# Turning q by VectorE in 32x32 blocks, one load per batch, in a linear attention followed by a softplus MLP

## The chip, the cores and the metric

The kernel runs on one core of a Trainium2 chip. The core has five engines with queues of their own: TensorE (PE in the profile, with its weight loads as PEld), VectorE (DVE), ScalarE (ACT), GpSimd (POOL) and SyncE (SP), which here issues nearly all transfers. Sixteen DMA engines move data between the device's memory and the core's memory. The metric is the device time of one execution in microseconds (us), as a median of several runs.

## The reference

```python
# q, k, v: (8, 8, 576, 64) = batch, head, row, column
kv = np.einsum('bhsd,bhse->bhde', k, v)
out = np.einsum('bhsd,bhde->bhse', q, kv)
rms = np.sqrt(np.mean(out * out, axis=-1, keepdims=True) + 1e-06)
out = out / rms * g_norm
x = out.transpose(0, 2, 1, 3).reshape(4608, 512)
h = x @ w_in                                               # (4608, 2048)
g = np.maximum(h, 0.0) + np.log1p(np.exp(-np.abs(h)))      # softplus
return g @ w_out                                           # (4608, 512)
```

The two weights arrive as 64-bit floats; all else is 32-bit. Each batch has 576 rows, that is four and a half tiles of 128 rows.

## The kernel before

**Tiles.** The 4608 rows are 36 tiles of 128. Three tiles make a block of 384 rows, so there are 12 blocks. The 2048 columns of the inner layer are 16 chunks of 128.

**Exactness.** Products of the MLP are made from three rounded factors of each operand, so each logical product is three matmuls. The factors of a weight (`divide`) and of x (`split`) are made by ScalarE and VectorE in turn: a high part, a low part, and a third that is combined from both.

**Attention.** `kv_of(b)` loads k and v of a batch and multiplies them on TensorE (L479), then copies the result block-diagonally into `kv_diag`: one half by ScalarE (L486), the other by VectorE (L487). `rows(t)` treats a tile of 128 rows: q is loaded with one row per partition (L401), turned by TensorE in four 128x128 transposes into the `tp` bank (`turn_q`, L497), copied by ScalarE into `qT` (L522), multiplied by `kv_diag` (`out_rows`, L503), squared by ScalarE (L527), summed by VectorE (L507), epsilon added by VectorE (L508), raised to the power -1/2 on Pool (L511), and multiplied by VectorE (L514). For the first six tiles (`AT_ONCE`) x is then turned by TensorE (`turn_x`, L519) and split at once out of PSUM; ScalarE also copies it (L535) to be stored (L536). For all other tiles VectorE turns x in blocks of 32x32 (L544) and four transfers with runs of 32 floats store it so that it lies fully turned in device memory (L547). Later phases load it again (L556, `x_again`) and split it.

**Steps.** A step is one block with one chunk. `step(s)` makes h by 12 matmuls (`mm1`, L578), softplus on ScalarE (L598), a high part (L600, ScalarE), a low part and a third (L589 and L593, VectorE), and nine matmuls into the three sums of the block (`mm2`, L585). There are 192 steps, in three phases set by `ENDS`: in each phase every block does its share of chunks. Between phases the sums are stored (L629) and added back (L623, L625). `PLACES` = 8 chunks of weights fit at a time; a weight whose place comes free too late is converted early and spilled to device memory (`w_spill`, L330).

**Order.** Nothing is scheduled by hand. Every piece of work is a `Task` with an engine, an estimated time, what it follows, a position, and the slots of rings (buffers) that it takes and gives back. `Plan.order` simulates the engines and picks for each the task with the smallest position among those that could start soon; the programs of all engines are written out in that order. Positions come from the step number and from the 40 numbers of `P0` (when weights are fetched and converted, how far ahead x, k, v and q are worked on). The rings say how many buffers there are: two for q, three for gv, two for sq. Each engine runs its list strictly in order, and so does SP with its transfers, each of which waits on SP until its buffer is free. While the first step is not reached, the plan fills idle time of TensorE with matmuls of no use (`warm`, L683).

## Time and profile before

| | |
|---|---|
| median of 5 runs | 926.32 us (926.02 to 927.71) |
| the profiled execution | 926.02 us, its span 924.2 us |
| granted TensorE clock | 1.00 |
| TensorE busy | 911.6 us of the span |
| VectorE busy | 624.9 us |
| ScalarE busy | 441.9 us |
| Pool busy | 64.0 us |
| transfers by SP's queue | 132.68 MB, 51.4% of the 16 engines' span |

A line of a group names the line of the program, the engine, the operation, what is written and read, the shape and the count; then busy time, mean duration in ns, the idle time of the engine just ahead of it and who ended that. A line of a timeline gives the start in us from the start of the span, the duration, and the same names; `x8` are eight like instructions in a row. Matmuls overlap, so what one costs is seen from one start to the next. A transpose of fp32 counts as one matmul, and an ordinary fp32 product as two (160 products with k and v stand as 320).

### The profile page before, as it was taken

The numbers are of one execution on the slowest core, as the hardware profiler recorded it, in microseconds if no ns is written. First come the engines' busy times: TensorE is split into PE (matmuls) and PEld (weight loads), VectorE is DVE, ScalarE is ACT, GpSimd is POOL, SyncE is SP. The second block draws the span as 40 slices with busy tenths as digits, with TensorE's granted clock in tenths as the row PEclk, the third lists the DMA queues.
The fourth block names the chain that finished last, engine by engine and source line by source line (L and its number), as shares of the span: only waits on it lengthen the run. The fifth ranks groups of instructions, "written<-read, shape, count | busy, mean of one in ns | idle before, by whom it ended". The sixth has DMA issues, their size and how long they took to land.

```text
span 924.2 us, 13404 instructions
## 1 busy us (share of the span) xinstructions
PE 911.6 (99%) x4897; PEld 825.0 (89%) x4897; DVE 624.9 (68%) x1075; ACT 441.9 (48%) x843; POOL 64.0 (7%) x42
## 2 busy tenths in 40 slices
PE   7999999999999999999999999999999999999998
PEld 5799899999999999999999989999999999999997
DVE  6988859886567764778688887584455555454553
ACT  5877547665445444655556453353333333333231
POOL 0322311111210220000000000000000000000000
PEclk9999999999999999999999999999999999999999
DMA  9998798676666634333455565522333333332221
GB/s 247 232 253 207 187 228 204 175 175 155 162 162 190 145 87 123 95 111 118 157 171 160 174 203 173 169 98 86 103 103 103 102 103 103 103 103 85 81 76 67
DMA packets 248033, 133.53 MB, mean 144 GB/s; under 512 B 149152, under 2 KB 220832, under 8 KB 247968
## 3 DMA queue, kind: packets, MB, share of 16 engines
q1 hardware_dynamic: 247808, 132.68, 51.4%
q8 instruction: 38, 0.62, 0.3%
q14 instruction: 27, 0.22, 0.1%
q10 hardware_dynamic: 160, 0.00, 0.0%
HBM read 92.80 MB, written 39.85 MB: 144 GB/s over the span
## 4 chain that ended last, share of the span: by engine, by line
PE 97%; DVE 1%; ACT 1%; DMA 0%; issue 0%; ACTq 0%; DVEq 0%
PE h L578 44%; PE s L585 43%; PE o L503 3%; PE o L479 3%; PE tp L497 2%; DMA g_col<-in_g_norm_dram 0%; PE s L503 0%; PE tp L519 0%; PE h L683 0%; DVE t L295 0%; PE h L363 0%; PE h L362 0%; DVE p L308 0%; DVE w L311 0%; ACT L649 0%
## 5 line engine op out<-in xcount | busy, mean ns | idle before, releaser
L578 PE MATMUL h<-xv,w 128*128 128x384 f32 x2304 | 436.1, 338 | 0.0
L585 PE MATMUL s<-w,gv 128*128 128x512 f32 x1728 | 432.9, 394 | 0.0
L578 PEld LDWEIGHTS h<-xv,w 128*128 128x128 f32 x2304 | 405.2, 188 | 14.1 <-issue 0.7
L585 PEld LDWEIGHTS s<-w,gv 128*128 128x128 f32 x1728 | 320.4, 188 | 58.1 <-DVE gv L593 0.2
L598 ACT ACTIVATE g<-h 128x384 f32<-128x384 f32 x192 | 94.3, 491 | 352.1 <-PE h L578 350.1
L589 DVE TENSOR_TENSOR gv<-g,gv 128x384 fp32r<-128x384 f32 x192 | 106.7, 556 | 173.0 <-ACT gv L600 172.4
L593 DVE SCALAR_TENSOR_TENSOR gv<-gv 128x384 fp32r<-128x384 f32 x192 | 106.9, 557 | 5.8
L600 ACT ACTIVATE gv<-g 128x384 fp32r<-128x384 f32 x192 | 100.8, 525 | 7.9 <-PE s L585 2.6
L419 DVE SCALAR_TENSOR_TENSOR xv<-xt,g_col,xv 128x512 fp32r<-128x512 f32 x102 | 76.2, 747 | 19.0 <-ACT xv L416 18.8
L416 ACT ACTIVATE xv<-xt,g_down 128x512 fp32r<-128x512 f32 x102 | 72.4, 713 | 26.8 <-DMA xt<-x 26.6
L511 POOL TENSOR_TENSOR r<-r,half 128x8 f32<-128x8 f32 x36 | 63.3, 1758 | 276.9 <-DVE r L508 276.9
L423 DVE SCALAR_TENSOR_TENSOR xv<-xv 128x512 fp32r<-128x512 f32 x108 | 74.5, 690 | 3.0
L479 PEld LDWEIGHTS o<-kvt,kvt 128*128 128x128 f32 x256 | 33.4, 196 | 4.7 <-issue 3.5
L479 PE MATMUL o<-kvt,kvt 128*128 128x128 f32 x256 | 34.7, 280 | 3.0 <-DMA kvt<-in_v_dram 3.0
L503 PE MATMUL o<-kv_diag,qT 128*128 128x128 f32 (+1 forms) x296 | 36.9, 276 | 0.0
L503 PEld LDWEIGHTS o<-kv_diag,qT 128*128 128x128 f32 (+1 forms) x296 | 34.5, 180 | 1.5 <-issue 0.7
L507 DVE TENSOR_REDUCE r<-x 128x8 f32<-128x512 f32 x36 | 24.4, 678 | 16.1 <-ACT x L527 15.9
L522 ACT COPY qT<-tp 128x512 f32<-128x512 f32 x36 | 21.0, 582 | 27.0 <-PE tp L497 26.9
L625 DVE SCALAR_TENSOR_TENSOR qT<-s,kvt 128x512 f32<-128x512 f32 x36 | 24.6, 687 | 13.7 <-PE s L585 9.8
L625 DVE SCALAR_TENSOR_TENSOR qT<-s,scale,kvt 128x512 f32<-128x512 f32 x12 | 9.0, 752 | 29.5 <-PE s L585 29.5
L527 ACT ACTIVATE x<-o 128x512 f32<-128x512 f32 x33 | 19.7, 596 | 16.3 <-PE o L503 14.4
L295 DVE SCALAR_TENSOR_TENSOR t<-sq,t 128x512 f32<-128x512 bf16 x32 | 22.1, 690 | 5.3 <-ACT sq L279 3.7
(71 smaller groups left out, 482.7 us busy)
## 6 DMA issues: line engine op xcount, KB each, us to landing
xt<-x SPq DMA_DIRECT2D x102, 256.0 KB, 3.3
kvt<-part SPq DMA_DIRECT2D x72, 256.0 KB, 4.3
part<-xg SPq DMA_DIRECT2D x36, 256.0 KB, 2.5
part<-qT SPq DMA_DIRECT2D x36, 256.0 KB, 2.4
raw<-in_moe_w_in_dram SPq DMA_DIRECT2D x16, 512.0 KB, 4.6
kvt<-in_k_dram SPq DMA_DIRECT2D x64, 128.0 KB, 4.3
kvt<-in_v_dram SPq DMA_DIRECT2D x32, 256.0 KB, 4.4
raw<-in_moe_w_out_dram SPq DMA_DIRECT2D x16, 512.0 KB, 4.6
```

Of the source, the lines that this page charges most:

```text
L416: nc.scalar.activation(cols(0, F32R), x.tile, func=AF.Identity, scale=g_down)
L419: nc.vector.scalar_tensor_tensor(out=cols(1, F32R), in0=x.tile, scalar=g_col, in1=cols(0), op0=ALU.mult, op1=ALU.subtract)
L423: nc.vector.scalar_tensor_tensor(out=cols(2, F32R), in0=cols(1), scalar=-RADIX, in1=cols(0), op0=ALU.mult, op1=ALU.add)
L479: nc.tensor.matmul(kv[:, i if tail else p], lhsT=l, rhs=r, start=(p == 0 and i == 0), stop=tail, skip_group_check=True)
L503: nc.tensor.matmul(pairs(y[r0:r0 + n], p), lhsT=qT.tile[:, p, r0:r0 + n], rhs=kv_diag[b % 2][:, p], start=(p == 0), stop=True, skip_group_ ...
L511: nc.gpsimd.tensor_tensor(out=r.tile, in0=r.tile, in1=half, op=ALU.pow)
L578: nc.tensor.matmul(hp, lhsT=w_in.tile[:, i, kd * P:(kd + 1) * P], rhs=xv.tile[:, i, kd], start=(m == 0), stop=(m == 3 * KD - 1))
L585: nc.tensor.matmul(mine[i].tile, lhsT=gv.tile[:, m, i * P:(i + 1) * P], rhs=w_out.tile[:, m], start=(c == cs[0] and m == 0), stop=(c == cs ...
L589: nc.vector.tensor_tensor(out=gv.tile[:, 1], in0=g.tile, in1=gv.tile.bitcast(F32)[:, 0], op=ALU.subtract)
L593: nc.vector.scalar_tensor_tensor(out=gv.tile[:, 2], in0=f32[:, 1], scalar=-RADIX, in1=f32[:, 0], op0=ALU.mult, op1=ALU.add)
L598: a = add("ACT", 490, lambda: nc.scalar.activation(new(g, [P, NT]), h.tile, func=AF.Softplus, scale=1.0 + E), [a], s, [g], [h])
L600: a = add("ACT", 530, lambda: nc.scalar.activation(new(gv, [P, 3, NT], F32R)[:, 0], g.tile, func=AF.Copy, scale=DOWN), [a], s, [gv])
```

## The change

- **q.** For the first two batches q is loaded as before in natural order, but with the heads paired differently (head p with head p + 4), and turned by TensorE. From the third batch on (`b >= 2`) a batch's q is loaded as a whole by four transfers (`load_q`), each into 32 partitions and with runs of 32 floats (128 bytes, where the old runs had 256), so that the 32x32 blocks lie where the turned matrix wants them. VectorE then turns the blocks of a tile in one instruction straight into `qT`. One buffer `qa` holds a batch; the ring of two row tiles is gone. The first two batches' tiles lie in `qa` and in `kvt` slots. A tile across two batches is turned in two parts.
- **Heads.** With the new pairing, k is loaded by halves, and the matmuls of `out_rows` write two strips of 64 columns each.
- **kv_diag.** Both halves are copied by ScalarE.
- **Epsilon** is added on Pool ahead of the power.
- **x.** TensorE turns x of 12 tiles (`BY_PE`) instead of 6. The six new ones are still split after a reload from device memory, but their store has runs of 512 bytes and is one transfer instead of four.
- **Phases.** `ENDS` and the positions in `P0` are new; the bound for spilling is 12 steps instead of 30; gv has two buffers and sq one. Tasks can be made to follow the start of another (`follows`).

```diff
-    ENDS = [[0] * n_blocks, [4] * LATE + [6] * (n_blocks - LATE), [10] * n_blocks, [KF] * n_blocks]
+    ENDS = [[0] * n_blocks, [4]*4+[6]*8, [8]*4+[11]*8, [KF] * n_blocks]
...
-    P0 = [-53.0, -6.2, -18.3, -1.2, -9.1, 4.0, -38.9, 0.2, -43.0, -32.8, -31.7, -14.2, -15.7, -21.2,
-          2.8, -3.7, 1.0, -9.5, 7.0, 7.0, 7.0, 24.5, -0.5, 2.5, 2.0, 16.5, -13.0, 4.5, 16.5, 21.5, 27.0,
-          42.5, 44.0, 66.5, 72, 80, 88, 96.5, 102.0, 3]
+    P0 = [-44.5, 1.3, -27.8, -10.7, -15.1, 4.5, -20.4, -2.8, -54.5, -31.8, -31.7, -9.2, -25.2, -1.2,
+          27.3, -6.2, 3.0, -12.0, 8.5, 9.5, 5.0, 21.5, -1.5, 2.5, 2.5, 27.0, -6.5, 13.0, 9.0, 44.5,
+          49.5, 67.5, 56.5, 71.5, 95.5, 100.5, 115.0, 112.0, 116.5, 9.0]
+    BY_PE = 12
...
-    rings = dict(xv=2, gv=3, g=2, raw=2, lf=1, sq=2, t=1, p=1, w=1,
-                 tail0=1, tail1=1, xt=2, kvt=6, q=2, qT=2, x=2, xg=2, r=2,
+    rings = dict(xv=2, gv=2, g=2, raw=2, lf=1, sq=1, t=1, p=1, w=1,
+                 tail0=1, tail1=1, xt=2, kvt=6, qa=1, qT=2, x=2, xg=2, r=2,
...
-        if c < PLACES or first_step[c] - last_step[c - PLACES] > 30:
+        if c < PLACES or first_step[c] - last_step[c - PLACES] > 12:
...
+    def load_q(b):
+        q_slots[b], q_loads[b] = slot("qa"), []
+        pos = x_pos(first_tile[b] + 1) - EARLY[7]
+        def run(e, c):
+            if not (e or c):
+                new(q_slots[b], [P, NP * S])
+            r0 = BL * (2 * e + c)
+            nc.sync.dma_start(
+                out=q_slots[b].tile[r0:r0 + BL].rearrange("j (i d) -> j i d", d=BL),
+                in_=q[b, e * NP:(e + 1) * NP, :, BL * c:BL * (c + 1)].rearrange("p (i j) d -> j (p i) d", j=BL))
+        for e in range(2):
+            for c in range(2):
+                q_loads[b].append(add("SP", 450, lambda e=e, c=c: run(e, c), (), pos + 0.2 * (2 * e + c),
+                                      [q_slots[b]] if not (e or c) else [], [], 2000, behind=int(pos) - 3,
+                                      follows=q_loads[b][-1] if e or c else None))
...
-            add("DVE", 430, lambda: nc.vector.tensor_copy(kvd[D:, :, D:], bank.tile[D:, :, 1]), [last] + old, pos + 2.5, [], [bank])]
+            add("ACT", 360, lambda: nc.scalar.copy(kvd[D:, :, D:], bank.tile[D:, :, 1]), [last] + old, pos + 2.5, [], [bank])]
...
-                    nc.tensor.matmul(pairs(y[r0:r0 + n], p), lhsT=qT.tile[:, p, r0:r0 + n], rhs=kv_diag[b % 2][:, p],
+                    nc.tensor.matmul(y[r0:r0 + n, p::NP], lhsT=qT.tile[:, p, r0:r0 + n],
+                                     rhs=kv_diag[b % 2][:, p].rearrange("r (h d) -> r h d", d=D),
...
-            nc.vector.tensor_scalar(out=r.tile, in0=r.tile, scalar1=EPS, scalar2=None, op0=ALU.add)
         def root():
+            nc.gpsimd.tensor_scalar(out=r.tile, in0=r.tile, scalar1=EPS, scalar2=None, op0=ALU.add)
             nc.gpsimd.tensor_tensor(out=r.tile, in0=r.tile, in1=half, op=ALU.pow)
...
-        a = add("PE", 440, turn_q, [ld], pos - 1, [tp], [q_s])
-        a = add("ACT", 590, lambda: nc.scalar.copy(new(qT, [P, NP, P]), tp.tile), [a], pos - 1, [qT], [tp])
+        for b, r0, n, s0 in parts(t):
+            if b >= 2:
+                if b not in q_slots:
+                    load_q(b)
+                turned.append(add(
+                    "DVE", 690 if n == P else 420, lambda b=b, r0=r0, n=n, s0=s0: nc.vector.transpose(
+                        out=part_of_qT(n, r0),
+                        in_=q_slots[b].tile.rearrange("k (p s) -> k p s", p=NP)[:, :, s0:s0 + n]),
+                    q_loads[b], pos - 1, [qT] if not r0 else [], [q_slots[b]], follows=turned[-1] if turned else None))
+                continue
...
-        if t < AT_ONCE:
+        if t < BY_PE:
             a = add("PE", 440, turn_x, [a], pos + 0.5, [xp], [x])
-            split(0, t, xp, a, pos + 0.5)
+            if t < AT_ONCE:
+                split(0, t, xp, a, pos + 0.5)
...
-        ot = slot("xg" if ph == 0 else ("qT", "x", "q")[t % TB] if ph == LAST else "qT")
+        ot = slot("xg" if ph == 0 else ("qT", "x", "xg")[t % TB] if ph == LAST else "qT")
```

## Prediction

> **What bounds the kernel now.** I read the page's head first, then the chain, the groups, a table by stage, and the timeline of the start.
>
> ```profile
> span 924.2 us, 13404 instructions
> PE 911.6 (99%) x4897; PEld 825.0 (89%) x4897; DVE 624.9 (68%) x1075; ACT 441.9 (48%) x843; POOL 64.0 (7%) x42
> PE 97%; DVE 1%; ACT 1%; DMA 0%; issue 0%; ACTq 0%; DVEq 0%
> PE h L578 44%; PE s L585 43%; PE o L503 3%; PE o L479 3%; PE tp L497 2%; DMA g_col<-in_g_norm_dram 0%; PE s L503 0%; PE tp L519 0%; PE h L683 0%; DVE t L295 0%; PE h L363 0%; PE h L362 0%; DVE p L308 0%; DVE w L311 0%; ACT L649 0%
> ```
>
> The chain that ends last is TensorE for 97% of the span, so work taken from TensorE is worth its full price and work on other engines costs nothing until TensorE must wait for it. L497, the turning of q, stands on that chain with 2%. The prices, from the groups:
>
> ```profile
> L497 PE MATMUL tp<-ident_r,q 128*128 128x128 f32 x144 | 21.7, 273 | 1.7 <-DVE xv L419 1.0 <-PE h L363 0.4 <-ACT qT L522 0.3
> L522 ACT COPY qT<-tp 128x512 f32<-128x512 f32 x36 | 21.0, 582 | 27.0 <-PE tp L497 26.9
> L544 DVE STREAM_TRANSPOSE xg<-x 128x512 f32<-128x512 f32 x30 | 21.2, 708 | 5.6 <-DMA x<-xg 5.2
> L508 DVE TENSOR_SCALAR r<-r 128x8 f32<-128x8 f32 x36 | 6.2, 172 | 1.2
> L511 POOL TENSOR_TENSOR r<-r,half 128x8 f32<-128x8 f32 x36 | 63.3, 1758 | 276.9 <-DVE r L508 276.9
> masks.py:199 POOL TENSOR_SCALAR_AFFINE_SELECT kv_diag<-kv_diag 128x128 f32<-128x128 f32 x1 | 0.3, 292 | 0.1
> ```
>
> Matmuls overlap, so what a turn costs TensorE is read from starts. In the timeline around 224 us:
>
> ```profile
> 221.79 2.45 PE L585 MATMUL s<-w,gv 128*128 128x512 f32 x10
> 224.08 0.60 PE L497 MATMUL tp<-ident_r,q 128*128 128x128 f32 x4
> 224.51 1.06 PE L479 MATMUL o<-kvt,kvt 128*128 128x128 f32 x8
> ```
>
> The reader should see 224.08 to 224.51: four transposes hold TensorE for 0.43 us, not 4 x 273 ns. The start is another regime:
>
> ```profile
> 0.00:20.00 20.00, 14.17 (x64) 10.33 (x64) 12.60 (x25) 10.95 (x20) 0.70 (x6) 1.00 0.91 240
> 20.00:40.00 20.00, 17.44 (x115) 13.62 (x114) 17.50 (x32) 16.13 (x33) 5.39 (x3) 1.00 1.04 255
> 80.00:100.00 20.00, 20.00 (x117) 17.60 (x116) 18.58 (x35) 12.53 (x25) 5.75 (x4) 1.00 0.67 165
> ```
>
> ```profile
> 41.42 0.71 PE L683 MATMUL h<-ident_r 128*128 128x512 f32 x2
> 42.05 2.32 PE L578 MATMUL h<-xv,w 128*128 128x384 f32 x12
> ...
> 41.74 0.69 DVE L423 SCALAR_TENSOR_TENSOR xv<-xv 128x512 fp32r<-128x512 f32 x1
> ```
>
> The first fence is the table by stage (stretch, length, then busy time of PE, PEld, DVE, ACT, POOL, clock, DMA share, GB/s), the second the timeline of the start. From 20 to 40 us VectorE is busy 17.5 of 20 us, ScalarE 16.1, and the DMA engines are full. The first step (L578) starts at 42.05 us, just as VectorE makes the last factor it needs (L423, from 41.74). Useful TensorE work before that is 16.2 us (the groups at their start-to-start times); the rest is waiting, padded by warming matmuls (L683). After 42 us TensorE never visibly waits, apart from one wait of 0.6 us and some 80 ns at changes of kind.
>
> **The change, part by part, against the profiled execution's 926.02 us** (span 924.2 and 1.8 around it; the median of the five runs, 926.32, is 0.3 higher).
>
> *TensorE work.* Turning q took 36 groups of four; 8 full ones and 2 of half width stay (two batches, with the tile on their border turned in two halves). That is 27 fewer. Six tiles of x more are turned by TensorE: +6. Net 21 x 0.43 = 9.0 us less. The bounds of one group are 0.36 (three starts of 109 ns and a last one of 28, without the gap at the change) and 0.46 (the chain's 1.8% of 924.2 over 36): 7.6 to 9.7. The matmuls of the steps stay 2304 and 1728, since the new limits of phases only move chunks between phases, and the partial sums stored and added back stay 72 and 72. The product with kv writes two strips of 64 columns instead of 128 together: same columns, taken as free.
>
> *VectorE.* 27 tiles' worth of block transposes of q (24 full, 6 half) at 0.708: +19.1 us. Off it go six block transposes of x (-4.2), 36 additions of epsilon (-6.2) and eight kv_diag copies of 0.427 (-3.4). Net +5.3 on an engine with 299 us free. What counts is where. I added durations along each engine's instruction order in both programs, from the last factor of block 0 on. To the last factor of block 2, VectorE has 52.8 us of work before and 41.0 after, against 54.6 and 53.9 us that TensorE has until it wants it. The margin grows from 1.8 to 12.9 us; between 40 and 160 us the smallest margin of any matmul is 1.8 to 12 before and 10 to 20 after. So the added transposes sit under TensorE's steps, because weights moved from there to the start and to later. ScalarE loses 27 copies of 0.582 (-15.7) and gains six of x (+3.5) and eight of kv_diag (+2.9).
>
> *The start.* Here the order costs. Ahead of block 0's last factor VectorE now has 56 instructions from the first weight on, not 52: ten more of the weights' (+6.1 us), less one kv_diag copy, one reduction and four additions of epsilon (-1.8), together +4.3 us. TensorE's useful work ahead of it is 16.7 instead of 16.2 us, and 48 warming matmuls stand there instead of 39. Against the +4.3: VectorE idles 2.9 us between 9.3 and 42.4 us before (0.69 for ScalarE's high part, 0.80 for its low part, 0.55, 0.50 and others), and the new order puts the next weight's first two operations into the first of these gaps; I take 1.0 back. And L423's result is read only by the third part of the step, 1.4 us after its start, so 1.0 us was slack. That gives +2.3 us, with bounds 4.3 - 2.9 - 1.0 = 0.4 and 4.3.
>
> *Epsilon on Pool.* No row shows this addition there. Bounds: 0.10 us (Pool's small memsets) and 1.76 us (the power, L511). I take 0.3, as in masks.py:199, the only one-input arithmetic in the rows. With the power's 1.64 to 2.12 the chain from reduction to root is 1.9 to 2.4 us; VectorE has four other operations in between (2.5 us in the new order for tiles 0, 1 and 3), so nothing at 0.3, and 1.1 us per tile, 3.3 us for the three tiles ahead of the first step, at 1.76. The Trainium skill, "SBUF — State Buffer", section "Who interferes with whom", says that GpSimd and VectorE can lock each other out of a shared port for a whole instruction, which speaks against moving work to Pool. By that rule each tile could lose up to one VectorE instruction. What this trace shows is the power's spread of 0.5 us over 36.
>
> *q per batch.* One buffer (qa) serves all batches, so batch b+1 loads only after batch b's last transpose; SP's queue and then VectorE wait for it in order, with the gv operations of later steps behind. Four loads of 2304 packets of 128 bytes: the trace's packet records between 100 and 340 us have a mean of 13.6 ns for 128-byte packets (all of them stores) and 18.3 for 256, so 7.8 us over 16 engines, at most 10.5. The old q loads had 1.2 us of packets and landed in 4.4 us, so 3.2 for the rest: 11 to 13.7 us after release. VectorE's own work in between is 11.4, 11.3, 9.3, 11.8 and 4.3 us at the five changes of batch; at the 4.3 two steps of TensorE (13 us) pace it. So 0 to 4 us of VectorE idle at a change, under margins of over 10. I take 0.5 us in all, bounds 0 and 9. Over the whole, packets cost 14.2 us more for q, 4.8 less for six x tiles stored in 512-byte runs, and 5.9 less because four chunks are no longer spilled twice but two: +3.4 us on engines that are 0.67 busy at 80 to 100 us. The Trainium skill speaks against such loads: "VectorE: DVE Perf Modes", section "The three transpose paths", calls a plain DMA with transposing strides 19 times slower than the crossbar's. Were that so here, a load of 2 us would be some 37 us, a batch about 150, and the kernel hundreds of us slower. But the x stores make the same 128-byte scatter and land in 2.8 us (median); I go by them.
>
> *Rings.* gv falls from 3 to 2 and sq from 2 to 1. A step takes 4.18 us in the last phase and its way through ScalarE and VectorE 0.49 + 0.53 + 0.56 + 0.56 = 2.1, so two gv suffice; sq's wait is inside the start's bounds.
>
> Sum: 926.0 - 9.0 + 2.3 + 0.5 = 919.8 us for the profiled execution, 920.1 with the median's 0.3; I say 920.0.
>
> **Rivals.**
> 1. *Slower: q's single buffer.* If a batch lands later than about 16 us after its release, VectorE stands at the transpose longer than steps of gv last, and TensorE waits. At the upper packet price with the loads queued behind as much other traffic (10.5 + 10.5 + 3.2 = 24 us) five changes lose some 10 us beyond their cover of 9 to 13, less 4 us of local slack: 5 x 7 = 35, or about 955 us in the extreme; the gain of 6 is gone at 1.3 us lost per change. For it: the DMA engines are 0.66 to 0.75 busy to 320 us. Against: they are not full, and SP's order spreads the four loads.
> 2. *No change: the start eats it.* +4.3 us and 3.3 from Pool leave 926.0 - 9.0 + 7.6 + 0.5 = 925.1. For it: nine more warming matmuls. Against: Pool's rows of simple operations are short.
> 3. *The start recovers.* At 0.4 us and 9.7 saved: 926.0 - 9.7 + 0.4 = 916.7; also the 80 ns gaps beside turned groups go (20 x 0.08 = 1.6): 915.1.
> That the change doesn't do what it says is excluded: the counts above are of the built program.
>
> **How the numbers follow.** A measurement here tells about 0.2% from no change, 1.9 us: faster is under 924.5, slower over 928.2. Forecast (917.5 to 922.5) 0.52; rival 3 (below) 0.14; a smaller gain, from bounds of the start and Pool (922.5 to 924.5), 0.10; rival 2 (no change) 0.11; rival 1 0.13. So faster 0.76, same 0.11, slower 0.13. The range leaves out rival 1 and the ends: 914.5 to 926.5; the forecast's own is 917.5 to 922.5.
>
> **What would show it.** In the profile after: about 40 instead of 144 matmuls turn q, 48 turn x, and TensorE's chain still over 95%; first step at 42.5 to 46.5 us; Pool's epsilon near 0.3 us and no wait of the norm on Pool over 1 us; VectorE's wait for q's loads under 4 us at each of five changes and no wait of TensorE on gv there. It would be wrong if the first step came after 48 us, if TensorE waited on gv or on qT by more than 2 us in all after it, or if the four loads of a batch took over 16 us.

## The result: no change

The changed kernel takes 926.49 us (median of 27 runs, 925.15 to 931.06), the kernel before 926.59 beside it (49 runs, 925.94 to 928.85). The ratio is 1.0001, with a 95% interval of 0.9996 to 1.0007. The forecast was 920.0, its range 914.5 to 926.5. The profiled execution of the changed kernel took 924.86 us, 1.16 less than the one before and 1.6 less than its own median; its runs spread more than those of the kernel before, and the profiled one is faster than all 27.

The page of the changed kernel, in the order busy times, queue, chain, groups:

```profile
span 923.1 us, 13338 instructions
...
PE 907.6 (98%) x4826; PEld 818.7 (89%) x4826; DVE 628.6 (68%) x1055; ACT 432.7 (47%) x831; POOL 83.7 (9%) x78
...
q1 hardware_dynamic: 264992, 130.59, 54.5%
...
PE 93%; DMA 2%; DVE 2%; ACT 1%; POOL 1%; issue 0%; ACTq 0%; SPq 0%; DVEq 0%
PE h L642 43%; PE s L649 43%; PE o L524 3%; PE o L507 3%; DMA kvt<-in_v_dram 2%; POOL r L533 1%; DMA g_col<-in_g_norm_dram 0%; PE tp L541 0%; ACT w L357 0%; PE tp L579 0%; DVE w L317 0%; PE h L747 0%; DVE xv L441 0%; DVE x L536 0%; PE h L369 0%
...
L532 POOL TENSOR_SCALAR r<-r 128x8 f32<-128x8 f32 x36 | 15.1, 421 | 245.4 <-DVE r L529 245.2
...
L554 DVE STREAM_TRANSPOSE qT<-qa 128x512 f32<-128x512 f32 (+1 forms) x30 | 19.0, 646 | 18.5 <-PE o L524 8.4
```

TensorE's work fell, but its share of the chain went from 97% to 93%: transfers of v, VectorE and Pool now stand on it. The queue's packets take 54.5% of the sixteen engines' span and not 51.4%, although 2.1 MB fewer are moved.

The table by stage (stretch, length, busy time of PE, PEld, DVE, ACT, POOL, clock, DMA share, GB/s):

```profile
20.00:40.00 20.00, 18.75 (x113) 14.14 (x113) 17.98 (x30) 17.18 (x34) 7.33 (x6) 1.00 1.05 242
40.00:60.00 20.00, 18.89 (x127) 16.40 (x126) 15.42 (x26) 13.99 (x28) 5.60 (x7) 1.00 1.08 210
...
80.00:100.00 20.00, 19.41 (x131) 17.60 (x130) 12.87 (x22) 11.08 (x21) 5.76 (x6) 1.00 0.75 212
...
140.00:160.00 20.00, 19.07 (x114) 17.61 (x114) 14.64 (x26) 8.37 (x17) 5.83 (x4) 1.00 1.20 184
```

The same stretches before the change:

```profile
40.00:60.00 20.00, 20.00 (x136) 18.07 (x136) 18.12 (x33) 15.44 (x31) 5.21 (x3) 1.00 0.94 240
...
140.00:160.00 20.00, 20.00 (x119) 18.52 (x118) 18.09 (x34) 14.34 (x30) 3.31 (x2) 1.00 0.86 208
```

From 40 to 60 and from 140 to 160 us the DMA share is over one (1.08 and 1.20, before 0.94 and 0.86) while fewer bytes are moved (210 and 184 GB/s, before 240 and 208). A share over one means that packets overlap in time, so a packet's duration can hold waiting for others. TensorE is idle in these two stretches for 1.1 and 0.9 us; before, it was not idle in them at all.

The waits of the engines (what waited, for whom, us in total, times, longest):

```profile
PE o L507 <- DMA kvt<-in_v_dram: 5.0, 4, 2.7
...
PE h L369 <- ACT w L357: 1.3, 2, 0.9
PE o L524 <- DVE x L536: 0.9, 1, 0.9
```

```profile
DVE qT L554 <- PE o L524: 8.4, 7, 3.2
...
DVE qT L554 <- DMA part<-xg: 5.5, 1, 5.5
DVE x L536 <- POOL r L533: 5.0, 11, 1.6
...
DVE qT L554 <- issue: 3.1, 1, 3.1
...
DVE qT L554 <- DMA qa<-in_q_dram: 1.4, 1, 1.4
```

The timeline of TensorE at the first step:

```profile
43.16 1.16 PE L507 MATMUL o<-kvt,kvt 128*128 128x128 f32 x8 [0.60 <-DMA kvt<-in_v_dram]
44.15 1.06 PE L507 MATMUL o<-tail,tail 128*128 128x128 f32 x8
44.97 1.03 PE L747 MATMUL h<-ident_r 128*128 128x512 f32 x3
45.93 0.46 PE L579 MATMUL tp<-ident_r,kvt 64*128 64x64 f32 x4
46.31 2.35 PE L642 MATMUL h<-xv,w 128*128 128x384 f32 x12
...
61.98 1.13 PE L507 MATMUL o<-kvt,kvt 128*128 128x128 f32 x8 [1.22 <-DMA kvt<-in_v_dram]
```

The first step (L642) starts at 46.31 us, not at 42.05. Ahead of it stands the last part of the product of k and v of batch 1 (L507), which waited for v. The chain that the profile follows back from the first step holds this load in full (start, duration, what):

```profile
14.72 4.38 DMA kvt<-in_v_dram
...
38.43 4.68 DMA kvt<-in_v_dram
...
43.16 2.05 PE o L507 x16
```

Before the change, the chain from 12 us to the first step holds no transfer.

**Where the time went.** To see it in one measure I took each matmul's start to the next start and took off a price for its kind from the rows (0.1745 us for a matmul of a first half of a step, 0.2325 for one of a second half, 0.109 for a transpose, 0.112 for each half of an fp32 product with k, v or q, 0.231 for the weights' sums, nothing for warming). What is left is TensorE's time beyond its work, by stretch of the profile, in us (a negative number means that the prices are a little high):

| | work | beyond it, 0 to 60 | 60 to 200 | after 200 | execution |
|---|---|---|---|---|---|
| before | 898.0 | 22.8 | 0.2 | -2.3 | 926.02 |
| changed | 889.2 | 26.5 | 3.8 | -2.1 | 924.86 |
| difference | -8.7 | +3.7 | +3.6 | +0.2 | -1.16 |

(Some 7.4 us of each execution lie ahead of the first matmul and behind the last one's start.) So the 9 us less of TensorE's work are there; 3.7 went in the start and 3.6 in new waits between 60 and 200 us. The other 1.6 us, from the profiled execution to the median, are not in this profile, and no run shows where they go.

In the trace the four longest of the new waits lead back to a load of v (1.4 us at 60 us), a weight fetch for which ScalarE stood 4.1 and VectorE 3.3 us (0.7 at 87 us), buffers that stores had not yet given back (0.6 at 134 us), and a norm (1.1 at 146 us), after VectorE had stood 2.6 us for a transfer and a power on Pool took 3.07 us.

### The profile page after: what moved, and what is told of

Read it like the earlier page. It is cut to its first block, busy times and chain, and to the rows that moved or that the text cites. A ratio compares the mean times of both kernels' runs of the same rounds, so it can differ in the third digit from the quotient of the medians.

```text
span 923.1 us, 13338 instructions
## 1 busy us (share of the span) xinstructions
PE 907.6 (98%) x4826; PEld 818.7 (89%) x4826; DVE 628.6 (68%) x1055; ACT 432.7 (47%) x831; POOL 83.7 (9%) x78
## 3 DMA queue, kind: packets, MB, share of 16 engines
q1 hardware_dynamic: 264992, 130.59, 54.5%
## 4 chain that ended last, share of the span: by engine, by line
PE 93%; DMA 2%; DVE 2%; ACT 1%; POOL 1%; issue 0%; ACTq 0%; SPq 0%; DVEq 0%
PE h L642 43%; PE s L649 43%; PE o L524 3%; PE o L507 3%; DMA kvt<-in_v_dram 2%; POOL r L533 1%; DMA g_col<-in_g_norm_dram 0%; PE tp L541 0%; ACT w L357 0%; PE tp L579 0%; DVE w L317 0%; PE h L747 0%; DVE xv L441 0%; DVE x L536 0%; PE h L369 0%
## 5 line engine op out<-in xcount | busy, mean ns | idle before, releaser
L642 PE MATMUL h<-xv,w 128*128 128x384 f32 x2304 | 434.1, 337 | 0.0
L642 PEld LDWEIGHTS h<-xv,w 128*128 128x128 f32 x2304 | 406.3, 188 | 14.6
L533 POOL TENSOR_TENSOR r<-r,half 128x8 f32<-128x8 f32 x36 | 67.8, 1884 | 3.0
L507 PEld LDWEIGHTS o<-kvt,kvt 128*128 128x128 f32 x256 | 33.7, 196 | 7.5 <-issue 5.0
L507 PE MATMUL o<-kvt,kvt 128*128 128x128 f32 x256 | 35.2, 282 | 5.1 <-DMA kvt<-in_v_dram 5.0
L532 POOL TENSOR_SCALAR r<-r 128x8 f32<-128x8 f32 x36 | 15.1, 421 | 245.4 <-DVE r L529 245.2
L554 DVE STREAM_TRANSPOSE qT<-qa 128x512 f32<-128x512 f32 (+1 forms) x30 | 19.0, 646 | 18.5 <-PE o L524 8.4
```

The lines of the kernel that those rows point to most:

```text
L507: nc.tensor.matmul(kv[:, i if tail else p], lhsT=l, rhs=r, start=(p == 0 and i == 0), stop=tail, skip_group_check=True)
L533: nc.gpsimd.tensor_tensor(out=r.tile, in0=r.tile, in1=half, op=ALU.pow)
L642: nc.tensor.matmul(hp, lhsT=w_in.tile[:, i, kd * P:(kd + 1) * P], rhs=xv.tile[:, i, kd], start=(m == 0), stop=(m == 3 * KD - 1))
```

## The experiments

All medians with their ratio to the kernel before, run beside it, and from each profile when SP issued the last full load of v of batch 1, when the first step started, and TensorE's time beyond its work as above (us):

| | median | ratio to before [95%] | v issued | first step | 0 to 60 | 60 to 200 |
|---|---|---|---|---|---|---|
| before | | 1 | 33.8 | 42.0 | 22.8 | 0.2 |
| changed | 926.49 | 1.0001 [0.9996, 1.0007] | 38.4 | 46.3 | 26.5 | 3.8 |
| e1_long_q | 923.29 | 0.9962 [0.9948, 0.9976] | 39.5 | 47.6 | 27.8 | 0.3 |
| e2_eps_dve | 926.78 | 0.9998 [0.9989, 1.0007] | 39.3 | 48.1 | 28.3 | 2.9 |
| e3_q_by_pe | 938.45 | 1.0127 [1.0112, 1.0141] | 39.7 | 48.3 | 28.5 | 3.5 |
| e4_old_start | 930.09 | 1.0032 [1.0020, 1.0045] | 39.6 | 49.2 | 26.9 | 7.3 |
| e5_q_alone | 930.32 | 1.0039 [1.0027, 1.0051] | 33.6 | 46.1 | 29.3 | 11.3 |
| e6_pool_queue | 932.25 | 1.0070 [1.0051, 1.0089] | 39.3 | 49.0 | 29.1 | 3.9 |
| e7_short_mask | 928.07 | 1.0012 [1.0003, 1.0021] | 38.9 | 47.7 | 27.9 | 3.9 |
| e8_long_start | 922.44 | 0.9962 [0.9948, 0.9975] | 37.4 | 46.3 | 26.5 | 1.5 |
| e9_all_long | 921.13 | 0.9941 [0.9929, 0.9953] | 38.3 | 46.9 | 27.1 | 0.5 |
| e10_all_long_mask | 920.89 | 0.9935 [0.9924, 0.9947] | 37.9 | 46.2 | 26.4 | 0.6 |
| e11_old_pairs | 925.77 | 0.9992 [0.9983, 1.0001] | 38.1 | 46.2 | 26.4 | 7.8 |
| e12_raw_later | 926.03 | 0.9993 [0.9984, 1.0002] | 37.6 | 46.1 | 26.3 | 4.5 |
| e13_short_act | 927.05 | 1.0007 [0.9998, 1.0016] | 38.4 | 46.5 | 26.7 | 6.7 |
| e14_all_relieved | 919.89 | 0.9931 [0.9918, 0.9943] | 36.8 | 44.8 | 25.0 | 0.4 |
| e15_v_sooner | 922.77 | 0.9962 [0.9950, 0.9975] | 40.2 | 47.4 | 28.3 | 1.7 |
| e16_w_in_later | 925.61 | 0.9994 [0.9985, 1.0003] | 38.2 | 45.4 | 26.5 | 3.2 |
| e17_xt_slot | 926.55 | 0.9993 [0.9984, 1.0002] | 35.2 | 45.4 | 25.6 | 5.2 |
| e18_relieved_xt | 923.99 | 0.9960 [0.9948, 0.9973] | 34.0 | 44.8 | 25.1 | 4.8 |

A ratio of 0.0010 is 0.93 us; differences to the changed kernel below are taken from the ratios. Four kernels share the changed kernel's order and loads (itself, e2, e7, e13), and their profiles have the first step at 46.3, 48.1, 47.7 and 46.5 us: a difference of under 1.8 us in one profile's first step says little by itself. The kernels with longer runs (e1, e8, e9, e10, e14, e18) load the same bytes in a wrong order, and those with short masks (e7, e10, e13, e14, e18) do a part of the weights' work on 8 of 512 columns for the first four chunks; they price a part and can't replace the kernel.

### Are the waits after the start from q's small runs? (e1, e6)

e1_long_q, long runs for q:

```diff
-                in_=q[b, e * NP:(e + 1) * NP, :, BL * c:BL * (c + 1)].rearrange("p (i j) d -> j (p i) d", j=BL))
+                in_=q[b, e * NP + 2 * c:e * NP + 2 * c + 2].rearrange("p (j i) d -> (p j) (i d)", j=BL // 2).rearrange("j (i d) -> j i d", d=BL))
```

> The changed kernel with the four q loads of a batch reading the same number of bytes in one run of 9216 bytes per partition instead of 72 runs of 128 bytes; the order of all instructions and all waits stay, the values in qa are in a wrong order, so the output is not the reference's. In the changed kernel's profile a 128-byte packet of these loads took 18.7 ns on average (13.6 was priced) and SP was held up to 2.9 us by one issue. Theory A (the small packets crowd out k, v and x transfers, and TensorE's new waits after 46 us, 1.5 us at 60, 0.7 at 87, 0.6 at 134, 1.2 at 146, come from that): 2 to 3.5 us faster than the changed kernel, about 922 to 924, the waits on the v loads fall from 5.0 us to under 3. Theory B (the lost time is the longer weight work ahead of the first step, the transfers are covered): within 0.7 us of the changed kernel, first step still at 46 us.

The ratio fell by 0.0039, 3.6 us. The new waits from 60 to 200 us went from 3.8 to 0.3, though the first step came at 47.6 us. So the size of q's runs, with nothing else changed, makes the waits after the start. It does not make the late first step. From profile to profile the gain is 2.2 us (922.64 against 924.86): 3.4 less in waits, 1.3 more in the start; most of the rest of the 3.6 is that the changed kernel's median lies further above its profile (1.6 us, here 0.7). The waits on v fell only from 5.0 to 4.6 us, not under 3: those that are left stand ahead of the first step.

```profile
PE o L507 <- DMA kvt<-in_v_dram: 4.6, 4, 2.5
```

SP's timeline at the change to the fifth batch, in the changed kernel and then in e1_long_q (start, duration of the issue or of several in a row):

```profile
140.62 2.47 SPq L416 DMA_DIRECT2D qa<-in_q_dram  x2
...
145.01 3.64 SPq L416 DMA_DIRECT2D qa<-in_q_dram  x2
148.75 3.36 SPq L611 DMA_DIRECT2D x<-xg  x1
```

```profile
138.86 0.92 SPq L416 DMA_DIRECT2D qa<-in_q_dram  x2
...
140.32 0.96 SPq L416 DMA_DIRECT2D qa<-in_q_dram  x2
```

The four loads hold SP's queue for 6.1 us with runs of 128 bytes and for 1.9 us with runs of 9216; the store that follows waits its turn.

The packet records give the price. All 104448 packets of 128 bytes in the changed kernel have a mean of 16.3 ns, those of the stores alone (after 285 us) 13.6. With 55296 of them from q's loads, these took (104448 x 16.3 - 49152 x 13.6) / 55296 = 18.7 ns. It differs from stretch to stretch: all 128-byte packets together take 26.9 ns from 46 to 55 us, 13.3 from 55 to 62, 19.4 from 99 to 108 and 21.3 from 140 to 152. The DMA share in these is 1.04, 1.05, 1.32 and 1.38, so the share alone does not tell the duration. A batch is then 2304 x 4 x 18.7 / 16 = 10.8 us of the sixteen engines, not 7.8.

e6_pool_queue takes these loads off SP:

```diff
-            nc.sync.dma_start(
+            nc.gpsimd.dma_start(
                 out=q_slots[b].tile[r0:r0 + BL].rearrange("j (i d) -> j i d", d=BL),
```

> The changed kernel with the four q loads of a batch issued by Pool instead of SP, so that k, v and x transfers do not queue behind them on SP; same bytes and runs. If the waits after the first step come from the order in SP's one queue (an issue of these loads held SP for up to 2.9 us): 2 to 3 us faster than the changed kernel, as with long runs (923.3). If they come from the packets' time on the sixteen engines: within 1 us of the changed kernel. If issuing 2304 runs costs Pool's time, the powers behind it come late and it is 1 us or more slower.

It was 6.4 us slower than the changed kernel. The busy groups of Pool (busy us, mean ns, idle before) show what it paid:

```profile
L416 POOL DMA_DIRECT2D qa<-in_q_dram x24 | 28.1, 1172 | 14.4 <-DVE qT L554 14.2 <-DMA x<-xg 0.2
```

Each load takes Pool 1.17 us, and Pool stood 14.2 us for VectorE's last use of the buffer, with the powers of later tiles behind it in order. In its profile some 3 us of the loss lie after 200 us, where TensorE has a wait of 2.7 us (from 286 us on). The order in SP's queue alone is thus not settled by this run, since the load's new place brought a cost of its own.

### What is turning q by VectorE worth? (e3, e5)

e3_q_by_pe:

```diff
-            if b >= 2:
+            if b >= B:
```

> The changed kernel with q of all batches turned by TensorE, as it does for the first two (loaded in rows of 256-byte runs into kvt slots); the plan orders everything anew. TensorE gets 27 to 29 turned groups of 0.43 us more: +11.6 to +12.5 us. If q by VectorE brought new waits of 3 us after the first step (theory A): about 8 to 9 us slower than the changed kernel, 934 to 936. If it brought none: 11.6 us slower, 938. If turning q was hardly worth anything because TensorE waits for others anyway: under 4 us slower.

The ratio says 11.7 us slower than the changed kernel, the price of TensorE's work (902.3 against 889.2, 13.1 us) less 1.4. So in this order q by VectorE is worth nearly all that the prediction gave it, and the changed kernel without it is 1.3% slower than before. The positions were not chosen anew for it, so what another order would give is not shown.

e5_q_alone, the q part alone (`P0`, `ENDS`, `BY_PE = 6`, the bound of 30, epsilon and kv_diag as before; the smaller rings of gv and sq stay, and for the one sq buffer the fetch of one weight moves from position 2.8 to -3.8; cut):

```diff
-    ENDS = [[0] * n_blocks, [4]*4+[6]*8, [8]*4+[11]*8, [KF] * n_blocks]
+    ENDS = [[0] * n_blocks, [4]*4+[6]*8, [10] * n_blocks, [KF] * n_blocks]
...
-    P0 = [-44.5, 1.3, -27.8, -10.7, -15.1, 4.5, -20.4, -2.8, -54.5, -31.8, -31.7, -9.2, -25.2, -1.2,
+    P0 = [-53.0, -6.2, -18.3, -1.2, -9.1, 4.0, -38.9, 0.2, -43.0, -32.8, -31.7, -14.2, -15.7, -21.2,
...
-    BY_PE = 12
+    BY_PE = 6
```

> The q part alone: the changed kernel with the positions, the limits of the phases, the spilling bound of 30 steps, six tiles of x turned by TensorE, epsilon and half of kv_diag on VectorE as before the change. What stays of the change: q per batch turned by VectorE from the third batch on, the pairing of heads, gv with two buffers, sq with one (for that one sq buffer the fetch of one weight is moved from position 2.8 to -3.8). TensorE's work is 27 groups less than before, less the split ones: -11.5 us. If what was lost comes from the new positions and phases of the start: first step at 42 to 44 us and 916 to 918.5 us, the new waits of some 3 us after the first step included. If it comes from q's loads themselves and the smaller rings: 921 to 926 us, near the changed kernel.

It was 3.6 us slower than before, outside both expectations. TensorE's work fell as expected (886.6), but 11.3 us of waits came between 60 and 200 us and 6.5 more in the start. The longest of these waits, 2.4 us, is for a tile of q that VectorE turned at 178.33 us, right after the last load of its batch had landed (178.25); 1.3 us near 185 us are for v. Part of the 6.5 is a stretch of 6.8 us at half clock from 45.0 us on. So with the old positions q's part loses all its gain to waits; how much of the others q's loads and how much the smaller rings make is not told apart. In this plan q's part needs the new positions and phases.

### Do the smaller parts cost? (e2)

e2_eps_dve:

```diff
             nc.vector.tensor_reduce(out=new(r, [P, H]), in_=x.tile, axis=AX.X, op=ALU.add)
+            nc.vector.tensor_scalar(out=r.tile, in0=r.tile, scalar1=EPS, scalar2=None, op0=ALU.add)
...
-            nc.gpsimd.tensor_scalar(out=r.tile, in0=r.tile, scalar1=EPS, scalar2=None, op0=ALU.add)
```

> The changed kernel with only the addition of epsilon put back on VectorE, the plan's estimates and so the order of all else unchanged. Pool's addition took 421 ns on average and the norm waited 5.0 us in all for Pool (2.0 before the change). If the Pool part costs: the norm's wait falls to 2 to 3 us and the time by 0.5 to 1.5 us. If it is covered: within 0.5 us of the changed kernel; four more additions of 0.17 us ahead of the first step could put it 0.7 us later.

The same within the measurement: the 5.0 us in which the norm waits for Pool cost the kernel nothing that shows in its time. Not undone one by one were the copies of kv_diag on ScalarE, the six more tiles of x on TensorE and the smaller rings.

### What makes the first step late? (e4, e7, e8 to e18)

The prediction's reason was VectorE's order: ten more of the weights' operations, 4.3 us net. e7_short_mask takes 4.1 us of it away:

```diff
-                nc.vector.scalar_tensor_tensor(out=tf, in0=sq.tile, scalar=2.0 ** 64, in1=tf,
+                n = 8 if c < 4 else d_model
+                nc.vector.scalar_tensor_tensor(out=tf[:, :n], in0=sq.tile[:, :n], scalar=2.0 ** 64, in1=tf[:, :n],
```

> The changed kernel with VectorE's masking of the weights' underflow (0.69 us each) done on 8 of 512 columns for the first four chunks; order and waits stay. Seven of these lie ahead of the last factor of block 0, so VectorE has 4.1 us less work there and one more right after. If VectorE's chain of weight work sets the first step (theory B): first step 2 to 4 us earlier and the time 2 to 4 us lower. If the transfers of k, v and q set it: first step within 1 us and the time within 1 us.

The first step came at 47.7 us and the time did not fall. VectorE's work alone does not set the start; that theory falls.

e4_old_start puts the old positions of the first four chunks' weights back:

```diff
+    P0[:16] = [-53.0, -6.2, -18.3, -1.2, -9.1, 4.0, -38.9, 0.2, -43.0, -32.8, -31.7, -14.2, -15.7, -21.2, 2.8, -3.7]
     CONVERT, FETCH, EARLY, LATER = P0[:8], P0[8:16], P0[16:27], P0[27:]
```

> The changed kernel with the sixteen positions of fetching and converting the first four chunks' weights as they were before the change; the rest is ordered anew by the plan. Theory B (the weights' order ahead of the first step costs the full 4.3 us): first step at 42 to 44 us instead of 46.3, time 2 to 4 us lower, about 922.5 to 924.5. If the later weights are then missed by the steps after the first, the first step comes earlier and the time stays within 1 us.

First step at 49.2 us, and 2.9 us slower than the changed kernel. The old order of weights does not bring the old start back.

e8_long_start, the transfers of the start with other runs:

```diff
-                        nc.sync.dma_start(out=x[:, h::2], in_=src[:, h])
+                        nc.sync.dma_start(out=x[:, NP * h:NP * h + NP], in_=src[:, h])
...
-                    nc.sync.dma_start(out=natural(q_s, at_qa)[:n, e::2], in_=halves(q[b, :, s0:s0 + n], e))
+                    nc.sync.dma_start(out=natural(q_s, at_qa)[:n, NP * e:NP * e + NP].rearrange("s h d -> s (h d)"),
+                                      in_=q[b, e * NP, :NP * n].rearrange("(s i) d -> s (i d)", i=NP))
```

> The changed kernel with k of all batches and q of the first two loaded in runs of 1024 bytes instead of 256, same bytes, same order, other values (so the output is not the reference's). These loads are some 1.2 us of the sixteen engines each at 256 bytes and some 0.9 at 1024 by the rows (18.5 and 54.5 ns a packet). If transfers set the first step: the 4.6 to 6.8 us of waiting on v fall by half, the first step comes 1 to 3 us earlier and the time falls by 2 to 4 us. If VectorE's weight work sets it: first step within 1 us, time 0.5 to 1.5 us lower from the later waits alone.

3.6 us faster by the ratio, but the first step stayed at 46.3; what fell are the waits from 60 to 200 us (1.5). That the loads of k then make room for q's is likely, but not shown.

e9_all_long (e1 and e8 together) and e10_all_long_mask (with e7 as well) have no edits of their own.

> Both changes of runs together: the batch loads of q in runs of 9216 bytes, k of all batches and q of the first two in runs of 1024; same bytes, order and waits, other values, so the output is not the reference's. Alone they took 3.2 us (923.3) and 4.1 us (922.4) off the changed kernel. Theory C (all that was lost against the prediction is the small runs' time on the transfer engines, in the start and after it): about 919 to 920.5, waits after the first step under 1 us in all. If the two remove the same waits: 922 to 923.

> As e9_all_long, and the masking of the first four chunks' weights on 8 of 512 columns, 4.1 us less for VectorE ahead of the first step. In e7_short_mask this alone gave nothing (928.1 against 926.5). If transfers set the start alone: within 0.7 us of e9_all_long. If VectorE's weight work stands right behind the transfers as a second bound: 2 to 4 us below e9_all_long, first step at 42 to 44 us.

With all long runs the kernel takes 921.1 and with the short mask 920.9: 5.6 and 6.1 us under the changed kernel, close to the forecast. The first step is still at 46.9 and 46.2 us.

e11_old_pairs (cut to its core) loads a tile of q with one transfer; e12_raw_later moves one weight's fetch:

```diff
-                for e in range(2):
-                    nc.sync.dma_start(out=natural(q_s, at_qa)[:n, e::2], in_=halves(q[b, :, s0:s0 + n], e))
+                nc.sync.dma_start(out=natural(q_s, at_qa)[:n], in_=q[b, :, s0:s0 + n].rearrange("h s d -> s h d"))
```

```diff
+    P0[10] = -30.9
     CONVERT, FETCH, EARLY, LATER = P0[:8], P0[8:16], P0[16:27], P0[27:]
```

> The changed kernel with the first two batches' heads paired as before (2p with 2p+1), so that a tile of q is loaded by one transfer and not two, and k's last rows too; order and bytes are the same, runs stay 256 bytes. SP issues 11 transfers fewer ahead of the first step, at some 0.5 us each; in the changed kernel SP issues for 38.4 of the first 46 us (32.2 before). If SP's issuing sets the late v loads of the start: first step 1 to 3 us earlier, 923.5 to 925.5. If the packets' time on the engines sets them: within 0.7 us of the changed kernel.

> The changed kernel with one position changed: the third weight fetch stands behind the k and v loads of the third part of batch 0 and not ahead of them. In the changed kernel SP stands 3.5 us (5.9 to 9.7 us) at this fetch until ScalarE lets go of the buffer, with k and v of the third and fourth parts behind it (before the change: 2.4 us, with one load more of k already out). If that wait makes the start late: v of the last part of batch 0 lands 2 to 3 us earlier, the first step comes 1 to 3 us earlier, 923.5 to 925.5. If later transfers catch up with it: within 0.7 us of the changed kernel.

Both are 0.7 to 0.8 us under the changed kernel by the ratio, with intervals that overlap its own, and have first steps at 46.2 and 46.1 us. Neither SP's number of issues nor its wait for the third weight's buffer sets the start alone.

Then ScalarE's share of the weights against the late v, e13_short_act to e16:

```diff
-                nc.scalar.activation(new(sq, [P, d_model], BF16), raw.tile.bitcast(BF16)[:, :, 3],
+                n = 8 if c < 4 else d_model
+                nc.scalar.activation(new(sq, [P, d_model], BF16)[:, :n], raw.tile.bitcast(BF16)[:, :n, 3],
...
-                nc.scalar.activation(sq.tile, sq.tile, func=AF.Identity, scale=2.0 ** -126, bias=big,
+                n = 8 if c < 4 else d_model
+                nc.scalar.activation(sq.tile[:, :n], sq.tile[:, :n], func=AF.Identity, scale=2.0 ** -126, bias=big,
```

> The changed kernel with, for the first four chunks' weights, the squares, the mask and the overflow sum made on 8 of 512 columns: 4.1 us less for VectorE (as in e7_short_mask, which alone gave nothing) and 7 times some 1.1 us, 8 us, less for ScalarE ahead of the first step; order, waits and transfers stay. In the changed kernel ScalarE is busy 17.2 of 20 us from 20 to 40 us, and the turned q of tile 1 waits for its copy behind the next weight's work. Theory D (ScalarE's share of the weight work, not counted in the prediction, sets the start): first step at 42 to 44 us, time 2 to 4 us lower (922.5 to 924.5). Theory E (TensorE's written order: the last part of batch 1's kv stands ahead of the first step and its v is issued 4.6 us later than before, behind two more weight fetches): first step still at 46 to 48 us, time within 1 us.

> e13_short_act and e9_all_long together: long runs for all loads of q and k, and short squares, masks and sums for the first four chunks. e9_all_long took 921.1. Theory D: 2 to 4 us below it, about 917.5 to 919, first step at 42 to 44 us. Theory E: within 1 us of 921, first step at 46 us.

e13 with 8 us less for ScalarE and 4 less for VectorE: first step at 46.5, no faster. e14, with the long runs too: 919.9 us, first step at 44.8, 1.5 us earlier than in the changed kernel. This is within the 1.8 us by which one order's profiles differ; e18 below, relieved in the same way, has 44.8 too. The chain of e14 holds no transfer after 18.9 us, and yet its first step is 2.8 us later than before the change. So neither transfers nor one engine's weight work hold the start alone, and even with all relieved most of the delay stays.

e15_v_sooner and e16_w_in_later:

```diff
-            lds = [add("SP", ns, lambda src=src, s=s, load=load: load(src, s), (), pos - EARLY[6] + 0.5 * p, [s], [],
+            lds = [add("SP", ns, lambda src=src, s=s, load=load: load(src, s), (),
+                       pos - EARLY[6] + 0.5 * p - (6 if b == 1 and p == 3 else 0), [s], [],
```

```diff
+    P0[6] = 2.0
     CONVERT, FETCH, EARLY, LATER = P0[:8], P0[8:16], P0[16:27], P0[27:]
```

> The changed kernel with one change of position: k and v of the last full part of batch 1 are loaded six positions earlier, so ahead of the seventh weight fetch and of q of batch 1; all else follows the plan. Theory E: TensorE no longer stands at this v (43.0 us in the changed kernel), the first step comes 1 to 3 us earlier; what is then late is q of batch 1 or the seventh weight, so the time may fall by less, 924 to 926. Theory D: first step within 1 us of 46.

> The changed kernel with one position changed: the conversion of w_in of the fourth chunk goes from -20.4 to 2.0, behind the first step's own work, so ScalarE and VectorE have up to one weight less (some 3.5 and 4.8 us) ahead of the first step. Theory D: first step 1.5 to 3 us earlier, time 1 to 2.5 us lower if the fourth step does not then wait for it. Theory E: first step within 1 us, time within 1 us.

e15 is 3.6 us faster than the changed kernel and beats both kernels, 922.77 us, 0.9962 [0.9950, 0.9975] of before. But not for the reason expected: the plan moved another load of v back (issued at 40.2 us), and the first step came at 47.4. The gain lies later. Waits from 60 to 200 us fell from 3.8 to 1.7, and the second half of a step ran a little faster, as its group shows (the changed kernel's row first):

```profile
L649 PE MATMUL s<-w,gv 128*128 128x512 f32 x1728 | 434.6, 395 | 0.6 <-ACT xg L683 0.5
```

```profile
L649 PE MATMUL s<-w,gv 128*128 128x512 f32 x1728 | 432.3, 394 | 0.2 <-ACT xg L683 0.2
```

From start to start this is 229.5 against 231.1 ns between 400 and 900 us, 2.8 us over 1728 matmuls; e5_q_alone has it too (229.2), no other. Why is not known. e16 moved the first step to 45.4 us and the ratio by 0.7 us, less than the intervals are wide.

In the profiles the first step follows the issue of the last full load of v of batch 1 by 7 to 10 us, in all but e5, e17 and e18. That load is issued 4.6 us later than before the change. In the changed kernel two halves of a tile of q hold two of the six kvt buffers. The load waits on TensorE for a buffer, by the plan's order the one that the product started at 35.7 us frees, and SP comes to it only at 38.4 us, behind a seventh weight fetch. Ahead of it SP has issued 9472 KB with seven weights, before the change 8448 KB with five. e17_xt_slot gives the buffer back, e18_relieved_xt does so on top of e14:

```diff
-            q_s = q_slots[0] if at_qa else slot("kvt")
+            q_s = q_slots[0] if at_qa else slot("xt" if t == 4 else "kvt")
```

> The changed kernel with the two halves of q's tile on the border of batches 0 and 1 loaded into the two xt buffers, which are idle then, and not into kvt slots; the plan orders the rest anew. In the changed kernel these halves hold two of the six kvt slots, so the last full v load of batch 1 waits for a slot until the kv product at 35.5 us is done, behind the seventh weight fetch, and is issued at 38.2 us (33.6 before the change). In twelve of thirteen profiles the first step came 7.2 to 9.6 us after this issue. Theory E: v issued 2 to 4 us earlier, first step at 43.5 to 45 us; the time falls by 1 to 3 us unless the anew ordered rest gives it back (then the first step shows it). Theory D: first step within 1 us of 46.

> e14_all_relieved (919.9, first step at 44.6 us, v issued at 36.6) with the two halves of q in the xt buffers as in e17_xt_slot. Theory E: v issued at 33 to 34 us, first step at 41.5 to 43 us, as before the change. If the rest of the order stays undisturbed, 917.5 to 919. If the first step stays at 44.6 us or later, something other than v and the weights' work holds it and stays open.

The load went 3.3 us earlier in e17, and TensorE no longer stood for it. The first step came at 45.4 us, 1.0 earlier, and then stood behind something else. TensorE's timeline in e17, and then two lines of the kernel before:

```profile
38.56 1.07 PE L507 MATMUL o<-kvt,kvt 128*128 128x128 f32 x8
...
41.03 1.13 PE L507 MATMUL o<-tail,tail 128*128 128x128 f32 x8 [0.17 <-issue]
41.99 0.60 PE L541 MATMUL tp<-ident_r,x 128*128 128x128 f32 x4
...
44.97 0.46 PE L579 MATMUL tp<-ident_r,xt 64*128 64x64 f32 x4 [0.69 <-DVE xv L441]
45.35 2.35 PE L642 MATMUL h<-xv,w 128*128 128x384 f32 x12
```

```profile
39.06 0.66 PE L519 MATMUL tp<-ident_r,x 128*128 128x128 f32 x4
...
40.61 1.06 PE L479 MATMUL o<-tail,tail 128*128 128x128 f32 x8
```

The third tile's x is turned at 41.99 us (41.0 in the changed kernel, 39.06 before), and its way through ScalarE and VectorE back to the one `tp` bank ends at 44.97. In e17 the turn stands behind the product with v's tail (L507 at 41.03), which before the change came after it. The load of v's tail (a batch's last 64 rows) is issued at 38.00 us and lands 2.9 us later, just ahead of that product; before the change it was issued at 30.3. ScalarE then copies both halves of kv_diag (until 42.9 us) before it takes up the turned tile. In e17 the 1.0 us gained and more are lost to a new wait of 2.57 us for a norm at 68.7 us, and the time is that of the changed kernel. e18 is slower than e14 by 2.7 us, with the same wait (2.56 us) and a stretch at half clock behind it, first step 44.8 as there. So v's late load is one leg; the tail's load and the third tile's turn are the next, close behind. In the order of e17 the tail accounts for at most 1.0 us of the turn's delay, for VectorE makes that x only at 41.0 us. What makes the rest of the 2 to 3 us stays open.

## Why the prediction was wrong, point by point

- **TensorE's work: right.** -9.0 predicted, -8.7 by the counts in the profile at the rows' prices; 40 transposes of q (16 from `qa`, 24 from `kvt`) and 48 of x, as counted. e3 shows that q's part is worth 11.7 us.
- **q per batch, 0.5 us (bounds 0 to 9): the mechanism named was not the one that cost, and the term was mis-sized.** I looked at the single buffer. VectorE did stand for the loads, 1.4, 3.1 and 5.5 us at three of the five changes of batch (more than the 0 to 4 I gave), and from the last use of one batch to the first of the next were 12.6, 14.3, 13.4, 21.0 and 15.3 us (over 16 was named as wrong; the fourth load of that batch was issued 10 us after its first). But TensorE lost nothing there: at 246 and 284 us, where the two long waits are, it has no time beyond its work. What cost were the packets. I priced 128-byte loads by the rows of 128-byte stores (13.6 ns); they took 18.7, and 26.9 in one stretch. The total I gave as +3.4 us was, by the queue's share, 0.545 x 923.1 - 0.514 x 924.2 = +28 us of packet time, waiting included. And I priced only their waiting reader and put the other transfers' delay at nothing, because the engines were 0.67 busy: v, a weight and stores are queued with them. TensorE's waits from 60 to 200 us grew by 3.6 us where I had 0.5, and e1 takes 3.4 of them away.
- **The start, +2.3 us (bounds 0.4 to 4.3): the size was off and the reason wrong.** The first step was 4.3 us later, and later still in other profiles of the same order; TensorE's time beyond its work grew by 3.7 us there. That 4.3 is also the upper bound is chance, since I had it from VectorE's list, with 1.0 us of idle and 1.0 of slack given back. e7 shows that 4.1 us less of VectorE's work brings nothing, e13 the same with ScalarE's as well, e9 for the transfers' runs; with all together, in e14, the first step is 1.5 earlier. The step that failed is the count along one engine's order. SP's order was not counted: the `kvt` buffers that q's border tile takes, and the two more weight fetches ahead of v, for which TensorE stood in the changed kernel. But with v 3.3 us earlier (e17) the first step came only 1.0 earlier, so what makes most of the delay stays open.
- **The median, +0.3 us: mis-sized.** I took over the distance from profile to median of the kernel before. It is 1.6 us for the changed kernel. With 3.6 for 0.5, 3.7 for 2.3 and 8.7 for 9.0 this is the forecast's miss of 6.5 us but for 0.4.
- **Epsilon on Pool: right in effect.** 0.42 us and not 0.3, the norm waits for Pool 5.0 and not 2.0 us, once for 1.6 us (over 1 was named as not expected), and e2 finds no cost in the time. In the changed kernel's profile the wait of TensorE at 146 us stands behind that one; in e1 it is gone, with the epsilon still on Pool.
- **The rules of the skill.** The Trainium skill, "VectorE: DVE Perf Modes", section "The three transpose paths", was rightly not followed in its size: a batch landed 12 to 21 us after its release and not 150. The page ties its factor to a large innermost stride at the destination; these loads write runs of 32 floats, so the rule is not tested here. "SBUF — State Buffer", section "Who interferes with whom", on Pool's port: e2 shows no cost in the time; whether the two engines ever locked each other out was not measured.
- **Rivals.** The result is nearest to the second, "the start eats it" (925.1), with the start as it said and q's traffic in the place of Pool's 3.3 us. The first, a slower kernel by the single buffer, did not come about in the changed kernel; in e5, with the old positions, TensorE's wait of 2.4 us for a late batch is of its kind.

## What to carry to other kernels

Price a transfer by rows of the same direction, run length and traffic, and ask not only when its own reader gets it but what is queued with it: here loads that cost TensorE nothing at their own reader cost it 3.4 us of waits for what was queued with them. A late start can have several legs that end within a few microseconds; count the order of the queue that issues the transfers, buffers included, as well as the engines' orders, before crediting any one of them. A part of a change that saves its full price (q, 11.7 us) can still need a new order that has a cost of its own.

## What the runs showed of the hardware

**A wait of TensorE of 2 us can halve TensorE's clock.** In e13_short_act TensorE waited for v, and the next 3.4 us ran at half the granted clock. Its timeline, then its table by stage:

```profile
60.39 0.60 PE L544 MATMUL tp<-ident_r,x 128*128 128x128 f32 x4
62.99 1.98 PE L510 MATMUL o<-kvt,kvt 128*128 128x128 f32 x8 [2.01 <-DMA kvt<-in_v_dram]
64.63 2.49 PE L652 MATMUL s<-w,gv 128*128 128x512 f32 x6
```

```profile
60.00:63.00 3.00, 0.99 (x9) 0.75 (x7) 1.00 (x2) 1.04 (x3) 0.92 (x1) 1.00 1.11 275
63.00:66.00 3.00, 3.00 (x11) 2.76 (x12) 2.44 (x5) 1.57 (x4) 0.00 (x0) 0.51 0.61 112
```

The eight matmuls of L510 took 1.98 us after the wait, where such a group takes some 1.1. The clock's records have such a stretch of 3.41 us between 40 and 900 us in e4, e6, e11, e13 and e18 (6.8 in e5), in e11, e13 and e18 behind a wait of 2.0, 2.0 and 2.6 us; a wait of 2.57 us in e17 had none, and the changed kernel's profile, whose longest wait after the first step is 1.22 us, has none. In every profile with more than one such stretch, the one at the very end included, their starts lie whole multiples of 3.413 us apart (e4: 9.42, 16.25, 74.27 and 927.60 us). Cut into windows of that length and phase, the six windows from 40 to 900 us just ahead of these stretches have TensorE busy for 1.28 to 1.66 us; the emptiest with full clock in it and behind it has 1.61 (e17 from 67.0 us), the next 1.76. e17's wait lies across the border of two windows. In e5 half clock went on into a second window although TensorE was busy for 2.9 us of the first. So the records fit a clock that falls by how little TensorE does in one such window; the length of a wait alone does not decide. At half speed a stretch can cost up to 1.7 us on top of the wait; e11's profiled execution, which has one, took 929.19 us against its median of 925.77. This may be why the changed kernel's runs spread, but no run isolates it. The Trainium skill, "TensorE: Matmul & The Clock Gate", section "Part 1: The HAM clock gate (the "warmup" mystery)", gives the same length, a free-running window of about 3.4 us, and has the clock fall after an idle window of that length. The length and the free run agree with the records here; but a window need not be idle, for 1.28 to 1.66 us of work in it did not keep the clock up.

**Packets of one size differ twofold in duration.** The 13.3 to 26.9 ns of a 128-byte packet are above, with shares of 1.05 and 1.04 beside them. The Trainium skill, "DMA: Bandwidth & Descriptors", section "Why small descriptors are slow (HBM only)", gives a fixed overhead of about three cycles for a packet; by its count a packet of 128 bytes should take 7/11 of one of 256, as an estimate 11.8 ns by this case's 18.5. The measurement decides: stores come near it with 13.6, but a fixed part does not describe the 18.7 of q's loads. What sets their duration is not shown.
